# Turning keys and queries on TensorE in every batch of a top-k attention and ELU layer

## The chip, the cores and the metric

The kernel runs on one core of a Trainium2 chip. The time is device microseconds of one execution, the median over runs. The profile is of one further execution of the same program.

## The reference, cut to what matters

Attention over 8 batches, 8 heads, 576 tokens and head width 64, in which each query keeps the 32 largest of its 576 scores, and behind it a two-layer network with an ELU between (4608 tokens, widths 512, 2048, 512).

```python
scores = scale * np.matmul(q, k.transpose(0, 1, 3, 2))
kth = np.partition(scores, -top_k, axis=-1)[..., -top_k:-top_k + 1]
scores = np.where(scores >= kth, scores, -1000000000.0)
scores = scores - np.max(scores, axis=-1, keepdims=True)
attn = np.exp(scores)
attn = attn / (np.sum(attn, axis=-1, keepdims=True) + 1e-09)
attn_out = np.matmul(attn, v).astype(np.float32)
...
x = attn_out.transpose(0, 2, 1, 3).reshape(B * S, H * D)
h = x @ w_in
g = np.where(h > 0.0, h, np.exp(np.minimum(h, 0.0)) - 1.0)
return (g @ w_out).astype(np.float32)
```

## The kernel before, in words

**Steps.** Queries are taken in tiles of 128 rows, and heads in pairs. 576 rows make four tiles (`J = 4`) and a remainder of 64 rows, the "last queries", of which a step takes two head pairs at once. One step is one tile and one head pair; there are 18 steps a batch, 144 in all (`NS`). `first[b]` is the first step of batch b, here called f. `orders[b]` says in which order a batch takes its tiles; `(J,)` in it stands for the remainder.

**What a step does, by engine.** `scores` (L331) multiplies queries by keys on TensorE into two PSUM tiles `wide[0]` and `wide[1]`, and ScalarE evicts them (L348) into the tile `sc`. `select` finds the 32 largest of each row on VectorE: a MAX8 on the scores (L360), then three times MATCH_REPLACE8 (L367) and MAX8 (L374), for both heads. `mask` makes weights of them on ScalarE (L401, L402), `normalise` scales them on POOL (L412 to L417). The weights are then turned so that keys lie on partitions: in one step of three by `turn`, on TensorE (L437) with a copy by ScalarE (L438), and in the two others ("aside") by `split`, `write` and `cross`, which send 16-bit halves through a DMA transpose. `turn` puts eight of its nine chunks into the PSUM pool `ps_t` (two buffers) and the ninth into free columns of `wide[1]`. `attend` (L488) multiplies by the values and `finish` copies into `xT`.

**The network behind it** is cut into pieces (`ffn_pieces`): `hidden` (L563, evicted at L573 to L582) and `product` or `project` (L656, L591). A "gate" is the last step of the ELU, on POOL (L533) or VectorE (L535); gates are put in a list and `close_gates` issues them some pieces later. `feed`, four times a step, issues as many pieces as a budget planned from `due` allows. Strips of w_out (`tw`) are streamed from DRAM by SP (L698).

**The order of the work** is written out by hand, one program order for all engines, and each engine runs its part in order. In program step n stand: the scores of step n + 2; the selection of step n; the mask and normalise of step n - 1; the turn, or the writing of halves, of step n - 2; the cross of step n - 3. `todo` holds calls for the start of a step and `mid` for its middle.

**Keys and queries before a batch.** Scores need the head width on partitions, in a tile `kqT` (`kvpool`, five buffers). For batch 0, `load_qk` loads rows as they lie (four rows to a partition), and `transpose_qk` turns them on TensorE with nine 128x128 transposes for a head pair: the leftover rows into free columns of `wide[0]` (L299), eight chunks into `ps_t` (L310), copied by ScalarE (L302, L306, L316). For batches 1 to 7, `load_halves` (L240) loads 32-column halves, so that 32x32 blocks lie ready, and VectorE turns them with two STREAM_TRANSPOSEs (L294), each 128x576. The input tiles of these batches have one buffer each. `plan` gives, for each of the four head pairs, how many steps before f it is loaded and how many before f it is turned (`start_qk` announces it; `turn_qk` runs one part in the middle of a step and the rest at its end). `load_v` (L274, L281) loads the values.

Of the kernel before, what the change touches and what calls it, by code (L numbers as in the profile page):

```python
# [10 lines left out]
FP32 = mybir.dt.float32  # L11
# [72 lines left out]
def kernel(  # L84
# [25 lines left out]
    KEYS, QUERIES = R, R + S  # L110
    Q = 32
    NB = S // Q
    scale = 1.0 / float(D) ** 0.5
# [134 lines left out]
    def load_qk(b, hp, other=nc.sync):  # L248

        for name, src in (("k", k), ("q", q)):  # L250
            n, queue = (J + 1, nc.sync) if name == "k" else (J, other)
            t = ldpool.tile([P, n, 2, D], FP32, tag=name + "in", name=name + "in")
            if name == "k":
# [12 lines left out]
    def load_v(b, hp):  # L266

        t = kvpool.tile([P, 2 * J + 2, D], FP32, tag="vT", name="vT")
        for hh in range(2):
            h = 2 * hp + hh  # L270
            main = R * hh if b else 0
            end = JP if b == 0 else JP * (1 - hh)
            order = "(p j) d -> p j d" if b == 0 else "(j p) d -> p j d"
            nc.sync.dma_start(  # L274
                t[:, hh * J : (hh + 1) * J, :],
                v[b, h, main : main + JP, :].rearrange(order, j=J),
            )
            mine = slice(hh * R, (hh + 1) * R)
            other = slice((1 - hh) * R, (2 - hh) * R)
            nc.gpsimd.memset(t[other, 2 * J + hh, :], 0.0)  # L280
            nc.sync.dma_start(t[mine, 2 * J + hh, :], v[b, h, end : end + R, :])  # L281
        vT[b, hp] = t

    def transpose_qk(b, hp):
# [5 lines left out]
        kqT[b, hp] = d[:].rearrange("p c d -> p (c d)")  # L290
        if b > 0:
            for i, name in enumerate(("k", "q")):
# [38 lines left out]
    def scores(u):  # L331

        u.sc = scpool.tile([P, 2, S], FP32, tag="sc", name="sc")
        q0 = (QUERIES if u.t.b == 0 else S) + u.t.qt * P
        for half in range(2):
            for h, i, rows in u.heads:
                kq = kqT[u.t.b, h // 2]
                part = slice(i * D, (i + 1) * D)
                k0 = (KEYS if i == 0 and u.t.b == 0 else 0) + half * HS
                nc.tensor.matmul(  # L340
# [381 lines left out]
    for b in range(B):  # L722
# [4 lines left out]
        else:  # L727
            order = [(0,), (1, 2), (3,)]
        if b % 2 and b > 1:
            if len(order[0]) == 2:  # L730
                order = [(0,), (1,), (2, 3)]
            orders.append(order[:1] + [(J,)] + order[1:])
        else:
            orders.append([(J,)] + order if b % 2 else order + [(J,)])
        ends += [(b, qt) for qts in orders[b] for qt in qts if qt < J or b % 2]
# [7 lines left out]
    for b in range(B):  # L743
        first[b] = len(steps)
        tiles = []
        for qt in range(J + 1):
            r0 = b * S + (JP if qt == J else qt if b == 0 else qt * P)
            if qt == J:
                (blk, slot), c0, n = slots[b | 1, J], (b % 2) * R, R
                rows = slice(r0, r0 + R)  # L750
            else:
                (blk, slot), c0, n = slots[b, qt], 0, P
                rows = slice(r0, r0 + J * (P - 1) + 1, J) if b == 0 else slice(r0, r0 + P)
            c0 += slot * P
# [24 lines left out]

    todo, mid = {}, {}  # L780

# [3 lines left out]
    for b in range(1, B):  # L785
        f = first[b]
        plan = ((9, 5), (4, 3), (2, 1), (0, -1))
        if len(orders[b][0]) == 1:
            plan = ((9, 5), (4, 3), (2, 1), (0.5, 0))
        if b == 1:  # L790
            plan = ((7, 5), (4.5, 4), (3.5, 3), (2.5, 2))
        for hp, (ahead, ready) in enumerate(plan):
            if ahead % 1:
                mid.setdefault(f - int(ahead + 0.5), []).append((load_halves, (b, hp)))
            else:
                at(f - ahead, load_halves, b, hp)
            at(f - ready, start_qk, b, hp)
# [66 lines left out]
    for n in range(NS + 3):  # L864
# [39 lines left out]
        if done and done.aside:  # L904
            split(done, 0)
            write(done, 0)
        if prev:
            normalise(prev)
            if prev.aside:
                close_gates(1)  # L910
                split(prev, 1)
        if spare and n >= first[1] - 2:
            difference(*spare.pop(0))
        feed(n, 0.25)
        turn_qk(True)
        if n < 2:
            scores(ahead)
# [36 lines left out]
```

## Time and profile before

| | |
|---|---|
| median of 3 runs | 1578.12 us (1576.59 to 1578.77) |
| the profiled execution | 1579.89 us |
| its span, first to last instruction | 1577.8 us |
| granted TensorE clock, mean | 0.967 |
| busy: TensorE, VectorE, ScalarE, POOL | 1461.6, 1450.2, 1182.8, 995.4 us |
| DMA queue q1 (SP) | 447856 packets, 197.49 MB |

Times in the profile are in microseconds from the start of the span; "mean ns" is of one instruction. PE is TensorE's matmuls, PEld its weight loads, DVE VectorE, ACT ScalarE, POOL GpSimd, SP the engine that issues most DMAs. An fp32 matmul shows as two records, a transpose as one. In a group of instructions the figures are: count, busy time in all, mean of one, and the idle time of the engine just before them with what ended it. In a wait they are: time in all, number, longest. In a stretch they are the busy times of the engines with the number of instructions, the granted clock, the share of the DMA engines and GB/s.

### The profile page before, as it was taken

How to read it: one execution, taken by the hardware profiler on the slowest of the kernel's cores; microseconds unless marked ns; L12 is line 12 of the kernel's file. 1: busy time of each engine (PE TensorE's matmuls, PEld its weight loads, DVE VectorE, ACT ScalarE, POOL GpSimd, SP SyncE). 2: the span in 40 equal slices, each digit the busy share in tenths (PEclk: the TensorE clock that was granted, in tenths of full speed). 3: DMA queues.
4: the chain of work that ended last, by engine and by line, in shares of the span. 5: the costliest groups of instructions: out<-in, count | busy, mean ns of one | idle time of the engine just before them, and what ended most of it. 6: DMA issues, size and time to landing. Idle time of an engine off the chain costs nothing.

```text
span 1577.8 us, 28727 instructions
## 1 busy us (share of the span) xinstructions
PE 1461.6 (93%) x9598; PEld 1155.1 (73%) x9598; DVE 1450.2 (92%) x2976; ACT 1182.8 (75%) x2296; POOL 995.4 (63%) x1493
## 2 busy tenths in 40 slices
PE   4789989989999999998999898999999999999899
PEld 2467557657777778776777776788788778887786
DVE  6899999999999999999899989999999997999600
ACT  6897677769696868686777777687969786978542
POOL 4993466655757566757575665758666666676550
PEclk9879989999999999999999999899999999999999
DMA  8621444646757585566646475738674757563410
GB/s 236 200 82 23 92 109 132 146 113 147 210 116 204 109 191 137 155 154 146 170 137 180 109 190 128 193 81 214 132 207 98 211 115 197 116 195 95 146 55 33
DMA packets 472595, 224.98 MB, mean 143 GB/s; under 512 B 385920, under 2 KB 430976, under 8 KB 472448
## 3 DMA queue, kind: packets, MB, share of 16 engines
q1 hardware_dynamic: 447856, 197.49, 50.3%
q10 hardware_dynamic: 24592, 25.66, 4.8%
q8 instruction: 76, 1.25, 0.3%
q14 instruction: 71, 0.58, 0.1%
HBM read 108.00 MB, written 64.36 MB: 109 GB/s over the span
## 4 chain that ended last, share of the span: by engine, by line
PE 41%; ACT 25%; DVE 14%; POOL 9%; issue 6%; DMA 3%; SPq 1%; ACTq 1%; DVEq 0%; POOLq 0%
PE ops L656 18%; PE hps L563 9%; PE avps L488 6%; DVE wk L367 6%; PE scps L340 5%; DVE m L374 5%; ACT sc L402 4%; ACT sc L401 4%; ACT n L573 3%; ACT n L578 3%; ACT sc L348 3%; ACT gT L576 2%; ACT n L582 2%; POOL sc L417 2%; ACT planes L454 2%
## 5 line engine op out<-in xcount | busy, mean ns | idle before, releaser
L374 DVE MAX8 m<-wk 128x8 f32<-128x576 f32 x864 | 607.8, 743 | 0.0
L563 PE MATMUL hps<-xT,w_in 128*128 128x256 f32 (+1 forms) x2688 | 541.0, 357 | 0.9 <-ACT xT L515 0.7
L563 PEld LDWEIGHTS hps<-xT,w_in 128*128 128x128 f32 x2688 | 452.8, 194 | 69.3 <-issue 19.8
L367 DVE MATCH_REPLACE8 wk<-m,wk 128x576 f32<-128x576 f32 x576 | 422.3, 739 | 0.0
L402 ACT ACTIVATE sc<-sc,den 128x576 f32<-128x576 f32 x288 | 223.4, 776 | 91.4 <-POOL den L381 78.1
L417 POOL TENSOR_SCALAR sc<-sc,den 128x576 f32<-128x576 f32 x288 | 236.2, 827 | 15.0
L401 ACT ACTIVATE sc<-sc,m 128x576 f32<-128x576 f32 x288 | 223.1, 775 | 26.8 <-DVE m L374 26.8
L412 POOL TENSOR_SCALAR den<-den 128x2 f32<-128x2 f32 x144 | 32.6, 226 | 331.8 <-ACT sc L402 329.2
L656 PE MATMUL ops<-tw,gT 128*128 128x256 f32 x960 | 224.9, 387 | 17.5 <-POOL gT L533 10.3
L340 PE MATMUL scps<-kqT 64*128 64x288 f32 (+1 forms) x1280 | 203.7, 449 | 39.3 <-ACT et L438 19.7
L656 PEld LDWEIGHTS ops<-tw,gT 128*128 128x128 f32 x960 | 179.5, 191 | 52.4 <-POOL gT L533 12.6
L360 DVE MAX8 m<-sc 128x8 f32<-128x576 f32 x288 | 201.6, 740 | 12.4 <-ACT sc L348 11.8
L367 DVE MATCH_REPLACE8 wk<-m,sc 128x576 f32<-128x576 f32 x288 | 211.0, 739 | 0.0
L348 ACT ACTIVATE sc<-scps 128x576 f32<-128x576 f32 x288 | 171.1, 647 | 51.0 <-PE scps L340 26.5
L533 POOL TENSOR_TENSOR gT<-n,gT 128x512 f32<-128x512 f32 x136 | 173.3, 1276 | 54.7 <-ACT n L582 53.7
L488 PEld LDWEIGHTS avps<-et,vT 128*64 128x64 f32 x3200 | 167.5, 142 | 44.6 <-issue 31.8
L488 PE MATMUL avps<-et,vT 128*64 128x128 f32 (+1 forms) x3200 | 190.7, 274 | 5.5 <-ACT et L438 5.4
L340 PEld LDWEIGHTS scps<-kqT 64*128 64x128 f32 (+1 forms) x1280 | 109.1, 184 | 108.6 <-issue 30.4
L656 PE MATMUL ops<-w_out,gT 128*128 128x256 f32 x720 | 175.1, 399 | 0.0
L656 PEld LDWEIGHTS ops<-w_out,gT 128*128 128x128 f32 x720 | 143.1, 202 | 24.7 <-issue 3.1
L609 POOL TENSOR_TENSOR gT<-gT 128x1024 f32<-128x1024 f32 x60 | 141.9, 2366 | 21.8 <-PE ops L656 20.5
L573 ACT ACTIVATE n<-hps 128x512 f32<-128x512 f32 x144 | 85.0, 591 | 55.7 <-PE hps L563 37.0
(57 smaller groups left out, 1486.3 us busy)
## 6 DMA issues: line engine op xcount, KB each, us to landing
tw<-kept SPq DMA_DIRECT2D x240, 256.0 KB, 3.5
halves<-planes ACTq DMA_DIRECT2D x86, 288.0 KB, 2.9
halves<-planes SPq DMA_DIRECT2D x86, 288.0 KB, 2.9
raw<-in_moe_w_in_dram SPq DMA_DIRECT2D x16, 512.0 KB, 5.4
vT<-in_v_dram SPq DMA_DIRECT2D x64, 128.0 KB, 2.9
raw<-in_moe_w_out_dram SPq DMA_DIRECT2D x16, 512.0 KB, 4.1
out_dram<-osb SPq DMA_DIRECT2D x32, 256.0 KB, 3.1
kin<-in_k_dram SPq DMA_DIRECT2D x112, 72.0 KB, 2.8
```

The source lines that it names most:

```text
L340: nc.tensor.matmul(wide[i][rows, half, 0:HS], kq[part, q0 : q0 + u.t.ql], kq[part, k0 : k0 + HS], start=True, stop=True,)
L348: nc.scalar.activation(u.sc[:, i, :].rearrange("p (a s) -> p a s", a=2), wide[i][:, :, 0:HS], AF.Copy, scale=scale,)
L360: nc.vector.max(found[i], cur[i])
L367: nc.vector.match_replace(wk[i], found[i], cur[i], TAKEN)
L374: nc.vector.max(found[i], cur[i])
L401: nc.scalar.activation(sc, sc, AF.Prelu, scale=-1.0, bias=low, alpha=1.0 / STEEP)
L402: nc.scalar.activation(sc, sc, AF.Exp, scale=-STEEP, bias=gap, accum_out=u.den[:, i : i + 1])
L417: nc.gpsimd.tensor_scalar(u.sc[:, i, :], u.sc[:, i, :], rec[:, i : i + 1], den[:, i : i + 1], ALU.mult, ALU.mult,)
L488: nc.tensor.matmul(ps[i * D : (i + 1) * D, cols], vt[:, 2 * J + i if c == J else i * J + c, :], w, start=(c == 0), stop=(c == J),)
L533: nc.gpsimd.tensor_tensor(dst, n, dst, ALU.add)
L563: nc.tensor.matmul(blk.h[:, f % bank, :], w_in[:, i, f * P : (f + 1) * P], blk.xT[:, i, 0:n_tok], start=(i == 0), stop=(i == NC - 1),)
L656: nc.tensor.matmul(sums, x[:, f, :], w, start=opens and f == 0, stop=f == NG - 1, skip_group_check=not opens,)
```

## The change

Keys and queries of all batches are loaded by `load_qk` as rows and turned by `transpose_qk` on TensorE; VectorE turns none. A set `by_pe` holds the batches that are treated so, here all. The tile of the loads comes from the pool that the late batches use, with one buffer for each of the two tensors. With it go:

- Keys now stand in another order (four neighbouring rows to a partition), so values are loaded in that order too, and a tile's output rows have a stride of four.
- The plan of loads and turns becomes (8, 6), (6, 4), (4, 2), (2, 0) steps before f for the four head pairs, and loads are issued at the end of their step, by a new table `behind`, after the turns of that step. In batch 1 the first load stands in the middle of a step.
- In batch 1 the remainder comes second, as it does in the other odd batches.
- In all steady steps `close_gates(1)` is called ahead of `normalise`; before it was called behind it, and only in steps that go aside.

```diff
+    by_pe = set(range(B))
...
     def load_qk(b, hp, other=nc.sync):
 
+        keep = late["in"] if b else ldpool
         for name, src in (("k", k), ("q", q)):
             n, queue = (J + 1, nc.sync) if name == "k" else (J, other)
-            t = ldpool.tile([P, n, 2, D], FP32, tag=name + "in", name=name + "in")
+            t = keep.tile([P, n, 2, D], FP32, tag=name, name=name + "in")
...
-            main = R * hh if b else 0
-            end = JP if b == 0 else JP * (1 - hh)
-            order = "(p j) d -> p j d" if b == 0 else "(j p) d -> p j d"
+            main = 0 if b in by_pe else R * hh
+            end = JP if b in by_pe else JP * (1 - hh)
+            order = "(p j) d -> p j d" if b in by_pe else "(j p) d -> p j d"
...
-        if b > 0:
+        if b not in by_pe:
             for i, name in enumerate(("k", "q")):
                 src = loaded.pop((b, hp, name))[:].rearrange("p n d -> p (n d)")
                 nc.vector.transpose(kqT[b, hp][:, i * S : (i + 1) * S], src)
...
-        if b % 2 and b > 1:
+        if b % 2:
             if len(order[0]) == 2:
                 order = [(0,), (1,), (2, 3)]
             orders.append(order[:1] + [(J,)] + order[1:])
         else:
-            orders.append([(J,)] + order if b % 2 else order + [(J,)])
+            orders.append(order + [(J,)])
...
-                rows = slice(r0, r0 + J * (P - 1) + 1, J) if b == 0 else slice(r0, r0 + P)
+                rows = slice(r0, r0 + P)
+                if b in by_pe:
+                    rows = slice(r0, r0 + J * (P - 1) + 1, J)
...
-        plan = ((9, 5), (4, 3), (2, 1), (0, -1))
-        if len(orders[b][0]) == 1:
-            plan = ((9, 5), (4, 3), (2, 1), (0.5, 0))
+        plan = ((8, 6), (6, 4), (4, 2), (2, 0))
         if b == 1:
-            plan = ((7, 5), (4.5, 4), (3.5, 3), (2.5, 2))
+            plan = ((7.5, 6), (6, 4), (4, 2), (2, 0))
         for hp, (ahead, ready) in enumerate(plan):
+            load = load_qk if b in by_pe else load_halves
             if ahead % 1:
-                mid.setdefault(f - int(ahead + 0.5), []).append((load_halves, (b, hp)))
+                mid.setdefault(f - int(ahead + 0.5) + 1, []).append((load, (b, hp)))
             else:
-                at(f - ahead, load_halves, b, hp)
+                behind.setdefault(f - ahead, []).append((load, (b, hp)))
...
         if prev:
+            if steady:
+                close_gates(1)
             normalise(prev)
             if prev.aside:
-                close_gates(1)
                 split(prev, 1)
...
         turn_qk(True)
+        for fn, args in behind.pop(n, []):
+            fn(*args)
```

More of the change, by code (lines that the diff above doesn't have):

```diff
@@ L333, in scores @@
         u.sc = scpool.tile([P, 2, S], FP32, tag="sc", name="sc")
-        q0 = (QUERIES if u.t.b == 0 else S) + u.t.qt * P
+        q0 = (QUERIES if u.t.b in by_pe else S) + u.t.qt * P
         for half in range(2):
@@ L338, in scores @@
                 part = slice(i * D, (i + 1) * D)
-                k0 = (KEYS if i == 0 and u.t.b == 0 else 0) + half * HS
+                k0 = (KEYS if i == 0 and u.t.b in by_pe else 0) + half * HS
                 nc.tensor.matmul(
@@ L746 @@
         for qt in range(J + 1):
-            r0 = b * S + (JP if qt == J else qt if b == 0 else qt * P)
+            r0 = b * S + (JP if qt == J else qt if b in by_pe else qt * P)
             if qt == J:
@@ L778 @@
             u.group.due = n + 4 + u.aside
-    todo, mid = {}, {}
+    todo, mid, behind = {}, {}, {}
     def at(step, fn, *args):
```

## The prediction

> **What bounds the kernel now.** I read the page first: busy shares, then the chain that ended last.
>
> ```profile
> span 1577.8 us, 28727 instructions
> PE 1461.6 (93%) x9598; PEld 1155.1 (73%) x9598; DVE 1450.2 (92%) x2976; ACT 1182.8 (75%) x2296; POOL 995.4 (63%) x1493
> PE 41%; ACT 25%; DVE 14%; POOL 9%; issue 6%; DMA 3%; SPq 1%; ACTq 1%; DVEq 0%; POOLq 0%
> ```
>
> TensorE and VectorE are equally full over the span, so the shares do not say which one sets the pace. Busy time by stage does; I cut the stages at the first MAX8 of a step (L360).
>
> ```profile
> 1322.89:1477.13 154.24, 150.09 (x1067) 123.53 (x1066) 154.24 (x322) 123.53 (x246) 104.85 (x158) 1.00 0.55 150
> 713.35:722.99 9.64, 9.64 (x90) 8.09 (x88) 9.64 (x21) 7.35 (x15) 6.80 (x11) 1.00 0.16 44
> 702.39:713.35 10.96, 7.90 (x47) 5.67 (x47) 10.96 (x23) 10.09 (x20) 5.52 (x9) 1.00 0.61 125
> 1304.34:1322.89 18.55, 18.55 (x123) 15.23 (x122) 11.20 (x23) 11.92 (x24) 15.17 (x20) 1.00 0.91 229
> ```
>
> The columns are PE, PEld, DVE, ACT, POOL, clock, DMA share, GB/s. The first row is sixteen steps without a transpose (20 VectorE instructions in each): VectorE is busy for all 154.24 us, 9.64 a step, as in the single step of the second row. The third row is a step with one pair of STREAM_TRANSPOSEs: 10.96, so a pair costs 1.32. In the fourth a pair also waits for its load: 18.55 us, of which VectorE works 11.20. The groups by line and shape give the totals:
>
> ```profile
> L294 DVE STREAM_TRANSPOSE kqT<-kin 128x576 f32<-128x576 f32 x28 | 21.2, 757 | 12.3 <-DMA kin<-in_k_dram 12.3
> L294 DVE STREAM_TRANSPOSE kqT<-qin 128x576 f32<-128x576 f32 x28 | 20.7, 740 | 9.9 <-DMA qin<-in_q_dram 9.8
> ```
>
> So VectorE sets the pace, but how far behind it is TensorE? I measured the lead: from the end of a step's score eviction (L348, two instructions in one row) to that step's first MAX8. These rows of the timeline are of steps 91 and 119:
>
> ```profile
> 927.98 1.19 ACT L348 ACTIVATE sc<-scps 128x576 f32<-128x576 f32 x2 [0.58 <-PE scps L340]
> 956.79 1.40 DVE L360 MAX8 m<-sc 128x8 f32<-128x576 f32 x2
> 1219.12 1.17 ACT L348 ACTIVATE sc<-scps 128x576 f32<-128x576 f32 x2
> 1232.14 1.40 DVE L360 MAX8 m<-sc 128x8 f32<-128x576 f32 x2
> ```
>
> Step 91 has its scores 956.79 - 929.17 = 27.6 us early, step 119 only 1232.14 - 1220.29 = 11.9. In those 28 steps VectorE took 9.83 us a step (275.4/28) and the producers of scores 10.40 (291.1/28). VectorE lives there on a stock of finished scores; its wait in the 18.55 us step fills the stock again. A kernel that takes these waits away therefore meets TensorE next. Its own demand:
>
> ```profile
> 131.81 1.24 PE L340 MATMUL scps<-kqT 64*128 64x288 f32 x8
> 1457.42 1.24 PE L340 MATMUL scps<-kqT 64*128 64x288 f32 x8
> 131.80:1457.40 1325.60, 1257.63 (x8443) 997.35 (x8442) 1302.78 (x2680) 1024.54 (x1972) 856.37 (x1307) 0.97 0.59 147
> 1034.04:1283.50 249.46, 245.59 (x1635) 201.15 (x1634) 249.44 (x513) 202.40 (x390) 170.03 (x252) 0.99 0.61 153
> 1486.86:1577.80 90.94, 87.18 (x482) 71.75 (x479) 2.77 (x4) 33.71 (x68) 26.57 (x25) 0.99 0.12 38
> ```
>
> Between the scores of step 12 (131.81) and of step 143 (1457.42) lie 131 steps, with 9.60 us of busy TensorE each (1257.63/131). The next row is 25 steps, from the scores of step 101, in which the lead was short: TensorE 98.4% busy, clock 0.99 against 0.97 over the long stretch. In the last, after VectorE's end, TensorE drains what is left.
>
> **What goes from VectorE.** 28 pairs by 1.32 = 37.0 us, and the waits for loads, 12.3 + 9.8 = 22.1. Together 59.1: by VectorE alone the span would be 1577.8 - 59.1 = 1518.7.
>
> **What comes to TensorE and ScalarE.** Each of the 28 head pairs of batches 1 to 7 now needs nine 128x128 transposes and four copies.
>
> ```profile
> L437 PE MATMUL eps<-ident,sc 128*128 128x128 f32 x464 | 75.2, 288 | 13.9 <-POOL sc L417 13.2 <-ACT xT L515 0.7
> L437 PEld LDWEIGHTS eps<-ident,sc 128*128 128x128 f32 x464 | 58.3, 148 | 31.6 <-POOL sc L417 21.0 <-issue 2.2 <-ACT xT L515 1.7
> L310 PE MATMUL qkps<-ident,kin 128*128 128x128 f32 x16 | 4.2, 421 | 0.0
> L316 ACT COPY kqT<-qkps 128x512 f32<-128x512 f32 x8 | 4.5, 599 | 1.5 <-PE qkps L310 1.5
> L302 ACT COPY kqT<-scps 128x128 f32<-128x128 f32 x4 | 1.0, 259 | 2.4 <-PE scps L299 2.3
> L306 ACT COPY kqT<-scps 128x64 f32<-128x64 f32 x4 | 0.9, 220 | 0.0
> ```
>
> TensorE: 252 transposes. The same operation in the steady part (L437) adds 75.2/464 = 0.162 us each, so 40.8 us. Bounds: 58.3/464 = 0.126 by its weight loads (31.7), 4.2/16 = 0.26 as batch 0 runs it at the cold start (66). I take 0.162, the row of the steady part. ScalarE: 28 x (2 x 0.599 + 0.259 + 0.220) = 47.0 us. In the long stretch it was busy 1024.5 of 1325.6 us (77%); with 47 more in a shorter stretch some 83%. It has the room, but it works in order, and these copies queue behind the mask of the step before, which waits for VectorE.
>
> **New waits on TensorE.** The four transposes of keys and of queries use the two ps_t buffers that attend and turn use; the ninth (the leftover rows) goes into bank wide[0], which the scores of the same step fill and ScalarE must empty first. Behind that transpose stand the step's other PE work and the next scores. The nearest rows are the single-chunk turn into wide[1] and what the score matmuls wait for:
>
> ```profile
> PE scps L437 <- ACT sc L348: 23.1, 18, 1.9
> L437 PE MATMUL scps<-ident,sc 128*128 128x128 f32 x58 | 18.3, 316 | 24.2 <-ACT sc L348 23.1 <-POOL sc L417 0.8
>   ACT et L438: 44.9, 22
>   DVE kqT L294: 10.7, 3
> ```
>
> The first two say that 18 of the 58 single-chunk turns waited, 23.1 us in all, 0.40 a turn: 28 x 0.40 = 11.2 us. From the other side, the last line is what scores waited for VectorE's transposes, 10.7, and that goes. The two about cancel: +0.5. Ends: -10.7 if no turn waits; if each waits as the 18 did, 1.28, it is 28 x 1.28 - 10.7 = +25.
>
> **Loads.** Per head pair, eight transfers become six, issued at the end of a step (behind what that step queued on SP) two steps ahead of their turn, where the last pair had half a step.
>
> ```profile
> kin<-in_k_dram SPq DMA_DIRECT2D x112, 72.0 KB, 2.8
> kin<-in_k_dram SPq DMA_DIRECT2D x8, 128.0 KB, 4.8
> L256 SPq DMA_DIRECT2D kin<-in_k_dram x8: 549/629/851, 0.7 to 18.6; - x8
> SPq L240 <- DVE kqT L294: 27.2, 3, 16.0
> ```
>
> Issue takes 6 x 0.63 = 3.8 us on SP, landing 4.8 by the row loads of batch 0: 8.6, against one and a half steps (14.5). So I cost the loads at nothing; what hides them is the step between. With one input buffer each, SP can be held at a load until the last pair is turned, as it was 27.2 us in three places; the w_out strips and score halves are queued behind. If the cover is gone, the 22.1 us of waits fall on TensorE instead.
>
> **The smaller edits.** The gates now close ahead of the normalise in every steady step. POOL has time there, and a gate's input (L582) stands ahead of the mask on ScalarE:
>
> ```profile
> POOL den L412 <- ACT sc L402: 329.2, 116, 6.7
> L533 POOL TENSOR_TENSOR gT<-n,gT 128x512 f32<-128x512 f32 x136 | 173.3, 1276 | 54.7 <-ACT n L582 53.7
> ```
>
> POOL waits 329.2 us for the mask before its normalise; the gate falls into that wait. Taken at 0; at worst a normalise is 1.28 us later, which the lead covers, and at best the halves leave 1.28 earlier. In batch 1 the two leftover steps move behind four others: the same instructions, and pair 3 is turned two steps before its use; 0. Values load in key order and rows store with a stride, the same number of transfers; 0.
>
> **Sum.** TensorE: 1257.6 + 40.8 = 1298.4 of busy time between the two score groups. VectorE needs 131 x 9.64 = 1262.8 for those steps, less, so TensorE is the later one now. It should then run as in the 25 short-lead steps: 1298.4 x 0.97/0.99 = 1272.2 at their clock, over 0.984 (245.59/249.46) = 1292.9. Before it lie 131.8 us, behind it 1577.8 - 1457.4 = 120.4, unchanged since TensorE has the same work there and was busy for 87.18 of the last 90.94. 131.8 + 1292.9 + 120.4 + 0.5 = 1545.6 of span. The profiled execution took 1579.89, 2.1 over its span, and the median of the runs is 1578.12, so 0.3 over the span: 1546. By this sum 59 us are released on VectorE and some 32 arrive.
>
> **The rivals.**
> First, TensorE has the room and VectorE stays the bound. TensorE's busy time holds modelled ends of matmuls that nothing needs, and steps in which it waited for VectorE anyway; weight loads were busy only 1155.1 of 1577.8 us. Then all 59.1 arrive: 1518.7 + 0.3 = 1519. Against it: 10.40 against 9.83 in steps 91 to 119. The Trainium skill (Perfetto Trace Analysis, Identifying the Most-Contended Engine) says that matmul busy time is no good measure and that weight-load busy time is one: by that rule TensorE at 73% has headroom, and the time would be this rival's. The trace agrees in part: weight loads are 81% (201.15/249.46) even where the lead shrinks, so that TensorE is short of time before this measure is full.
> Second, slower: the turn holds TensorE at wide[0]. The ninth transpose waits for an eviction that stands behind ScalarE's other work, and the next scores wait until ScalarE has copied it out. Price per turn: 1.28 for the first and, in half of them, 44.9/22 = 2.04 for the second, together 2.30. The sum then has 28 x 2.30 = 64.4 in place of 0.5: 1610. It decides from (1577.8 - 1545.1)/28 = 1.17 us a turn. For it: ScalarE at 83%, in order. Against it: 40 of 58 single-chunk turns did not wait.
> Third, the change does not do what it says because the loads are late for TensorE as they were for VectorE: +22.1, 1568. SP's 27.2 speaks for it, the 14.5 us against it.
> Fourth, the clock falls in the transposes. At batch 0's 421 ns against 288 the 252 cost 40.8 x 421/288 = 59.6, so 1565. Against it are the 464 transposes at 288 between matmuls. The Trainium skill (TensorE: Matmul & The Clock Gate, Part 4: PE-mode transpose) holds that transposes do not count as activity for the clock gate, which speaks against the change; the 464 show no such loss.
>
> **How the numbers follow.** Forecast 0.52, room on TensorE 0.22, late loads 0.07, clock 0.03, slower at wide[0] 0.16. What a measurement of this kernel can tell is about 0.2%, 3.2 us. Of the rival at wide[0] I give 0.13 to slower and 0.03 to no change (about 1.17 us a turn); of the forecast's own spread 0.02 goes to no change. Faster 0.50 + 0.22 + 0.07 + 0.03 = 0.82, same 0.05, slower 0.13. The range goes from 1519 (the room on TensorE, which has too much chance to be left out) up past late loads and the forecast with every turn waiting (1546 + 25 = 1571, or 1546 + 66 - 40.8 = 1571 with the dear transposes) to no gain: 1519 to 1580.
>
> **What would show it.** Right: no STREAM_TRANSPOSE on VectorE and no waits for kin; steps of 9.64 without the 10.96 and 18.55 in the first half; a lead that shrinks to a few us, and MAX8 (L360) waiting for L348 in the last third; 252 more transposes at about 0.16; PE busy between 1476 (1461.6 + 40.8, at the better clock) and 1502, over 95% of the span; ScalarE busy near 1230. A lead that stays over 10 us to the end shows the first rival. Wrong: VectorE idle from batch 2 on behind scores, with TensorE waiting for L348 or for the copies of kqT by over 1.2 us a turn, or waits of TensorE for kin and qin; or PE busy over 1530.

## The result, and the profile after

The changed kernel takes 1583.36 us (median, 1580.81 to 1588.44) against 1574.46 us (1571.95 to 1578.77) for the kernel before in the runs beside it: ratio 1.0066, 95% interval 1.0053 to 1.0078. It is slower by some 10 us by the ratio; the forecast was 1546, faster by 2% than the 1578.12 us that it started from. The profiled execution took 1583.26 us, its span is 1581.4. From here on lines are those of the changed kernel; most stand two below those of before (scores L342, eviction L350, first MAX8 L362, mask L403 and L404, turn L439; the new turn is L301 and L312, with its copies at L304, L308 and L318).

The page after, first the busy shares, then the chain that ended last:

```profile
span 1581.4 us, 29155 instructions
PE 1473.1 (93%) x9850; PEld 1175.5 (74%) x9850; DVE 1415.2 (89%) x2920; ACT 1216.7 (77%) x2412; POOL 997.6 (63%) x1493
PE 47%; ACT 30%; POOL 10%; issue 6%; DVE 3%; DMA 2%; SPq 1%; ACTq 1%; POOLq 0%
```

VectorE has lost 35 us of work and has gone from the chain (14% before, 3% now). But its place was not taken by TensorE alone: ScalarE stands in the chain with 30% where it had 25%, though it is busy for only 77% of the span.

Stretches of the span (same columns as in the prediction). The first row is the stretch from the scores of step 12 to those of step 143, as it was quoted of before; the next two are VectorE's steps 11 to 73 and 74 to 143, cut where it first has to wait, the last is what lies behind VectorE's end:

```profile
131.80:1459.40 1327.60, 1267.30 (x8695) 1016.46 (x8694) 1283.71 (x2656) 1058.36 (x2088) 858.54 (x1307) 0.99 0.55 147
143.73:751.22 607.49, 578.13 (x4105) 455.75 (x4105) 607.46 (x1261) 487.92 (x962) 392.01 (x608) 0.99 0.55 146
751.22:1473.46 722.24, 688.78 (x4609) 563.49 (x4608) 678.37 (x1401) 571.57 (x1128) 474.70 (x707) 0.98 0.57 151
1473.46:1581.40 107.94, 101.73 (x590) 84.38 (x588) 2.77 (x4) 43.75 (x91) 33.83 (x41) 0.97 0.20 62
```

In the second row VectorE is busy for 607.46 of 607.49 us: 63 steps of 9.64, as forecast. In the third row it idles for 722.24 - 678.37 = 43.9 us, and 70 steps take 10.32 each. VectorE ends 13.4 us earlier than before (1473.46 against 1486.86), but what lies behind its end is 17.0 us longer (107.94 against 90.94). That is not new work: from the last scores to the end of the span it takes 122.0 us where it took 120.4. VectorE now ends 14.1 us after the last scores begin where it ended 29.4 us after them, since its stock is gone, and the last scores themselves come no earlier (1459.4 against 1457.4).

How the stock of finished scores is used up can be seen in the timeline, by a step's eviction (two instructions in one row) and the MAX8 that reads it, here for steps 20 and 75:

```profile
208.57 1.19 ACT L350 ACTIVATE sc<-scps 128x576 f32<-128x576 f32 x2 [0.62 <-PE avps L490]
230.49 1.41 DVE L362 MAX8 m<-sc 128x8 f32<-128x576 f32 x2
...
762.69 1.19 ACT L350 ACTIVATE sc<-scps 128x576 f32<-128x576 f32 x2 [2.37 <-PE scps L342]
763.38 1.42 DVE L362 MAX8 m<-sc 128x8 f32<-128x576 f32 x2 [2.44 <-ACT sc L350]
```

Step 20 has its scores 230.49 - 209.76 = 20.7 us early; in step 75 VectorE starts as soon as the first of the two evictions has ended, having waited 2.44 us. That the lead would go was expected. The surprise is in what TensorE itself then waits for (waits: total, number, longest):

```profile
PE scps L342 <- ACT kqT L318: 30.3, 9, 8.4
PE scps L342 <- ACT et L440: 15.2, 9, 2.4
PE scps L301 <- ACT sc L350: 15.0, 10, 3.7
PE scps L439 <- ACT sc L350: 14.8, 13, 2.3
DVE m L362 <- ACT sc L350: 43.2, 20, 11.9
POOL gT L535 <- ACT n L584: 173.2, 71, 8.7
```

The four largest waits of TensorE are all for ScalarE. The two largest of the kernel before were so too (23.1 us at the single-chunk turn, 19.7 for the copy `et`); the first and the third row, all but 1.5 us of the latter, are what has come. In the first row, four waits with 12.3 us lie in the start-up; 18.0 us in five waits are new: the scores wait for the copy that hands over their own keys. Here is one of the five, in the timeline:

```profile
218.28 0.60 ACT L575 ACTIVATE n<-hps 128x512 f32<-128x512 f32 x1 [0.62 <-ACT planes L456]
218.78 0.59 ACT L578 ACTIVATE gT<-hps 128x512 f32<-128x512 f32 x1
219.25 0.63 ACT L580 ACTIVATE n<-n 128x512 f32<-128x512 f32 x1
219.92 0.63 ACT L584 ACTIVATE n<-n 128x512 f32<-128x512 f32 x1
220.45 0.57 ACT L318 COPY kqT<-qkps 128x512 f32<-128x512 f32 x1
221.07 2.29 PE L342 MATMUL scps<-kqT 64*128 64x288 f32 x8 [6.21 <-ACT kqT L318]
```

The copy takes 0.57 us, but it stands behind four instructions of the network's ELU, and these behind a half of the weights (L456); TensorE is idle for 6.21 us. ScalarE is not full; it has a line, and TensorE waits for something at the line's end.

### The profile page after: what moved, and what is told of

It is laid out like the page before. It is cut to its first block, busy times and chain, and to the rows that moved or that the text cites. A ratio compares the mean times of both kernels' runs of the same rounds, so it can differ in the third digit from the quotient of the medians.

```text
span 1581.4 us, 29155 instructions
## 1 busy us (share of the span) xinstructions
PE 1473.1 (93%) x9850; PEld 1175.5 (74%) x9850; DVE 1415.2 (89%) x2920; ACT 1216.7 (77%) x2412; POOL 997.6 (63%) x1493
## 3 DMA queue, kind: packets, MB, share of 16 engines
q1 hardware_dynamic: 360944, 197.48, 47.3%
## 4 chain that ended last, share of the span: by engine, by line
PE 47%; ACT 30%; POOL 10%; issue 6%; DVE 3%; DMA 2%; SPq 1%; ACTq 1%; POOLq 0%
PE ops L658 18%; PE hps L565 13%; PE avps L490 6%; PE scps L342 6%; ACT sc L404 5%; ACT sc L403 5%; ACT n L575 3%; ACT n L580 3%; ACT sc L350 3%; ACT gT L578 3%; ACT n L584 3%; POOL sc L419 2%; PE ops L593 2%; ACT planes L456 2%; POOL den L415 2%
## 5 line engine op out<-in xcount | busy, mean ns | idle before, releaser
L565 PE MATMUL hps<-xT,w_in 128*128 128x256 f32 (+1 forms) x2688 | 546.7, 359 | 0.6 <-ACT xT L517 0.6
L404 ACT ACTIVATE sc<-sc,den 128x576 f32<-128x576 f32 x288 | 223.4, 776 | 85.4 <-POOL den L383 71.7
L362 DVE MAX8 m<-sc 128x8 f32<-128x576 f32 x288 | 202.9, 747 | 49.9 <-ACT sc L350 43.2
L342 PE MATMUL scps<-kqT 64*128 64x288 f32 (+1 forms) x1280 | 203.1, 450 | 46.2 <-ACT kqT L318 30.3
L403 ACT ACTIVATE sc<-sc,m 128x576 f32<-128x576 f32 x288 | 224.0, 778 | 2.1 <-DVE m L376 2.1
L658 PE MATMUL ops<-tw,gT 128*128 128x256 f32 x960 | 221.1, 384 | 3.9 <-DMA tw<-kept 3.2
L350 ACT ACTIVATE sc<-scps 128x576 f32<-128x576 f32 x288 | 171.4, 649 | 52.0 <-PE scps L342 33.1
L342 PEld LDWEIGHTS scps<-kqT 64*128 64x128 f32 (+1 forms) x1280 | 109.9, 185 | 110.1 <-ACT kqT L318 33.1
L658 PE MATMUL ops<-w_out,gT 128*128 128x256 f32 x720 | 165.2, 383 | 0.0
L658 PEld LDWEIGHTS ops<-w_out,gT 128*128 128x128 f32 x720 | 135.5, 191 | 21.6 <-issue 4.0
L575 ACT ACTIVATE n<-hps 128x512 f32<-128x512 f32 x144 | 85.4, 593 | 63.2 <-PE hps L565 43.1
```

What stands on the lines that cost most here:

```text
L342: nc.tensor.matmul(wide[i][rows, half, 0:HS], kq[part, q0 : q0 + u.t.ql], kq[part, k0 : k0 + HS], start=True, stop=True,)
L350: nc.scalar.activation(u.sc[:, i, :].rearrange("p (a s) -> p a s", a=2), wide[i][:, :, 0:HS], AF.Copy, scale=scale,)
L362: nc.vector.max(found[i], cur[i])
L403: nc.scalar.activation(sc, sc, AF.Prelu, scale=-1.0, bias=low, alpha=1.0 / STEEP)
L404: nc.scalar.activation(sc, sc, AF.Exp, scale=-STEEP, bias=gap, accum_out=u.den[:, i : i + 1])
L565: nc.tensor.matmul(blk.h[:, f % bank, :], w_in[:, i, f * P : (f + 1) * P], blk.xT[:, i, 0:n_tok], start=(i == 0), stop=(i == NC - 1),)
```

## The experiments

The first four runs were to decide between three theories. **The bank:** the ninth transpose, into `wide[0]`, holds TensorE (the prediction's second rival). **Plain work:** only the 41 us of transposes count. **The gates:** closing them ahead of the normalise is the loss. When none of them fitted all four, two more came in. **ScalarE's line:** the 47 us of copies lengthen ScalarE's in-order line; what stands behind them comes late, evictions above all, and TensorE, which no longer has VectorE's slack in front of it, waits. **The handing over:** the scores wait for the copy of their own keys. All ratios are to the kernel before, with 95% intervals; 0.1% is about 1.6 us. The kernel before was timed anew beside each group of runs (its medians lie between 1574.46 and 1580.7 us), so kernels are compared by their ratios.

**1. The turn taken out** (`no_turn`). The loads, the gates and the new order stay.

```diff
+        if b > 0:
+            kqT[b, hp] = kqT[0, hp]
+            yield
+            return
         d = kvpool.tile([P, 4 * J + 3, D], FP32, tag="kqT", name="kqT")
```

> The changed kernel without the turn in batches 1 to 7: their scores use batch 0's turned keys and queries, loads stay. Bank theory (each turn holds TensorE some 1.6 us at wide[0], beside 41 us of transposes): both go, 1583 - 41 - 45 is under VectorE's own bound, so VectorE sets the time, 1519 to 1530. Plain work theory (only the 41 us of transposes count): about 1542. Gate theory (closing gates ahead of the normalise ties POOL to TensorE and is the loss): no better than 1555, since the gates stay.

Measured: 1538.63 us, ratio 0.9756 (0.9726 to 0.9786). Against the changed kernel's 1.0066 the turn costs 3.1%, some 49 us: more than the 40.8 us of TensorE's transposes if every one of them stood on the path. Of the three expectations the 1542 of plain work is nearest; the bank theory's 1519 to 1530 is not reached.

**2. The ninth transpose taken out** (`no_ninth`). In batches 1 to 7 the two small copies read the first chunk's PSUM tile; `wide[0]` is not used by the turn.

```diff
-        ps = wide[0][:, 1, HS : HS + P]
-        nc.tensor.transpose(
-            ps, srcs[0][:, J, :, :].rearrange("p h d -> p (h d)"), ident[:]
-        )
+        if b == 0:
...
+            if b > 0 and i == 0:
+                rest(ps[:, 0:P])
```

> The changed kernel without the ninth transpose in batches 1 to 7: the two small copies read the first chunk's PSUM tile instead of wide[0], so 64 leftover rows hold other rows' values. Bank theory: TensorE no longer waits for the eviction of wide[0], 28 x 1.2 to 1.6 us go, 1540 to 1552. Plain work theory: 28 x 0.16 = 4.5 us go, 1578. Gate theory: the same 1578.

Measured: 1587.95 us, ratio 1.0067 (1.0041 to 1.0094), the same as with the ninth. TensorE's waits in this kernel (its lines are six below those of the changed kernel):

```profile
PE scps L348 <- ACT kqT L324: 30.6, 9, 9.0
PE scps L445 <- ACT sc L356: 21.1, 17, 2.4
PE eps L445 <- ACT kqT L324: 6.3, 5, 2.3
PE scps L309 <- ACT sc L356: 1.5, 2, 0.7
```

The wait at the ninth transpose is gone (15.0 us in 10 in the changed kernel, 1.5 in 2 of the start-up now), and others for ScalarE have grown by nearly as much: the single-chunk turn from 14.8 to 21.1, a wait of the turn for the copy of the keys from 0.6 to 6.3. Part of the latter may come from the edit itself, since the two small copies now read a buffer of `ps_t`. The bank theory falls, and experiment 5 speaks against it too: there the wait at `wide[0]` stays (13.4 us in 10) and the kernel is faster than the one before. By these rows the wait is a place at which TensorE notices that ScalarE is late; without it TensorE notices later.

**3. The gates put back** (`gates_back`), where the kernel before had them.

```diff
-            if steady:
-                close_gates(1)
             normalise(prev)
             if prev.aside:
+                close_gates(1)
                 split(prev, 1)
```

> The changed kernel with close_gates(1) where it was: behind the normalise and only in steps that go aside. Gate theory: 1583 falls by 10 us or more. Bank theory and plain work theory: within 4 us of 1583.

Measured: 1600.47 us, ratio 1.0158 (1.0123 to 1.0193). The gate theory, by which this gains 10 us or more, falls: the edit that the prediction took at 0 is worth 0.9%, about 14 us, in the changed kernel.

**4. VectorE turns** (`dve_turn`), with the new gates, loads as early and the new order.

```diff
-    by_pe = set(range(B))
+    by_pe = {0}
```

> The changed kernel with by_pe = {0}: VectorE turns batches 1 to 7 again, with the changed plan of loads and turns, the gates and the order of batch 1 as changed. Bank and plain work theories: VectorE pays 28 x 1.32 = 37 us but no longer the 22 us of waits for loads, TensorE pays nothing: 1574.5 - 22 = 1552, at best. Gate theory: the gates hold it back, 1570 or more.

Measured: 1568.57 us, ratio 0.9937 (0.991 to 0.9963). All of the change but the turn, and the loads and the key order that belong to it, makes the kernel faster by 0.6%. That is between the two expectations, 1552 at best and 1570 or more.

**5, 6 and 9. The turn's parts alone.** `pe_only` keeps the 252 transposes and leaves the copies out; `act_only` keeps the copies, out of the loaded rows in SBUF, and leaves the transposes out; `act_aside` is `act_only` with the copies going to a spare tile that nobody reads, while the scores use batch 0's keys.

```diff
+        if b > 0:
+            flat = [x[:].rearrange("p n h d -> p (n h d)") for x in srcs]
+            nc.scalar.copy(d[:, 2 * J + 1 : 4 * J + 3 : 2 * J + 1, :], ...flat[0]...)
+            nc.scalar.copy(d[:, 0, :], flat[0][:, 0:R])
+            for i in range(2):
+                c0 = KEYS + i * (2 * J + 1) * D
+                nc.scalar.copy(kqT[b, hp][:, c0 : c0 + JP], flat[i][:, 0:JP])
+                yield
+            return
```

> The changed kernel with the 252 transposes of batches 1 to 7 but without the four copies a pair: scores use batch 0's turned keys and queries. Between no turn at all (1538.6) and the changed kernel (1583). TensorE-work theory: the transposes are the price, 41 us at most: 1570 to 1583. ScalarE theory (the price is 47 us of copies in ScalarE's queue, which delays the evictions that TensorE waits for): 1540 to 1555. Handing-over theory (the price is that scores wait for the last copy of a pair, 18 us of waits for kqT): about 1565.

> The changed kernel with the four copies a pair but without the transposes in batches 1 to 7: ScalarE copies the loaded rows as they lie, from SBUF, so keys and queries are not turned. TensorE-work theory: 1538 to 1545. ScalarE theory: 1570 or more. Handing-over theory: some 1555, since scores still wait for the last copy.

> The kernel act_only again, but its four copies a pair go to a spare tile that nobody reads; scores use batch 0's turned keys and queries, there are no transposes in batches 1 to 7. The same ScalarE time as act_only, and no score waits for a copy. ScalarE theory (47 us of copies delay everything behind them in ScalarE's queue): near act_only, 1575 to 1589. Handing-over theory (the loss is that scores wait for the copy of their own keys): near no turn at all, 1539 to 1548.

| kernel | in it, of the turn | us | ratio | over `no_turn` |
|---|---|---|---|---|
| `no_turn` | nothing | 1538.63 | 0.9756 (0.9726 to 0.9786) | |
| `pe_only` | transposes | 1556.87 | 0.9842 (0.9813 to 0.987) | 0.9%, 14 us |
| `act_aside` | copies that nobody waits for | 1566.92 | 0.9919 (0.9893 to 0.9944) | 1.6%, 26 us |
| `act_only` | copies that the scores wait for | 1589.16 | 1.0053 (1.0018 to 1.0089) | 3.0%, 47 us |
| changed | all | 1583.36 | 1.0066 (1.0053 to 1.0078) | 3.1%, 49 us |

The copies alone cost nearly what the whole turn costs; the transposes alone cost less than a third of it. The copies cost in two ways: 26 us when nobody waits for them, and 21 more as soon as somebody does. The 26 lie between what the two theories expected (36 to 50 us over `no_turn`, and at most 9), so each is right in part. The waits of TensorE in `act_only` show the second part; `act_aside` has no such row:

```profile
PE scps L354 <- ACT kqT L309: 28.8, 5, 8.3
PE scps L451 <- ACT sc L362: 24.5, 17, 2.4
PE scps L354 <- ACT et L452: 20.7, 13, 3.5
```

L309 is the copy of the keys: five waits, 28.8 us. The intervals of such differences are some 0.4% wide either way, so the third and the fourth row differ surely, but the parts add up only roughly (0.9% and 3.0% make more than 3.1%).

Waiting is not all that the copies cost. In the stretch from the scores of step 12 to those of step 143 (us, from the profiles):

| kernel | stretch | TensorE busy | idle | clock |
|---|---|---|---|---|
| `no_turn` | 1284.3 | 1239.3 | 45.0 | 0.99 |
| `pe_only` | 1301.5 | 1258.2 | 43.3 | 0.99 |
| `act_aside` | 1313.0 | 1249.6 | 63.4 | 0.98 |
| `act_only` | 1333.1 | 1253.9 | 79.2 | 0.97 |
| changed | 1327.6 | 1267.3 | 60.3 | 0.99 |

`act_only` has 34.2 us more of idle time than `no_turn`, and 14.6 us more of busy time for the same matmuls, at a lower granted clock; for `act_aside` it is 18.4 and 10.3. The mean clock was lower in each of their runs (0.960 to 0.972) than in any of `no_turn` and `pe_only` (0.977 to 0.981). Whether the waits bring the clock down was not tested. The changed kernel's clock did not fall, so the two costs are not to be carried over to it one by one.

**7. Copies earlier** (`whole_mid`): both parts of a turn in the middle of its step, where one stood in the middle and one at the end.

```diff
-            turn_qk()
+            turn_qk(True)
```

> The changed kernel with both halves of a pair's turn in the middle of the step (turn_qk(True) there), so that the copy of the queries stands ahead of the second mask on ScalarE. Handing-over theory: most of the 18 us of waits for kqT go, 1565 to 1572. TensorE-work theory: 1583 within 4. ScalarE theory: 1583 within 4, or slower, as more copies stand ahead of the mask.

Measured: 1583.74 us, ratio 1.0028 (1.0005 to 1.0051). By the ratio that is some 6 us better than the changed kernel, but the times (1583.74 and 1583.36) and the stretches between the two score groups (1328.4 and 1327.6) are the same, so that a gain is not shown; 1565 to 1572 was expected for the handing over. The wait of the scores for the keys goes from 30.3 us in 9 to 13.1 in 5, little more than the start-up's; but the turn of the weights now waits for the copy:

```profile
PE scps L342 <- ACT kqT L318: 13.1, 5, 8.7
PE eps L439 <- ACT kqT L318: 12.4, 6, 4.0
```

Two thirds of what went from the first came back in the second, because both use the two buffers of `ps_t`. A better place for the copies is not enough.

**8. A POOL step moved** (`spread_dve`): the difference at L383, on which the mask waits 71.7 us, computed by VectorE.

```diff
-        nc.gpsimd.tensor_tensor(
+        nc.vector.tensor_tensor(
             u.den[:, 2:4], u.last[:, :, 7], u.first[:, :, 0], ALU.subtract
```

> The changed kernel with the small subtraction `spread` (128x2) on VectorE instead of POOL, so that ScalarE's second mask no longer waits behind POOL's gates (71.7 us of waits in 45 places). If ScalarE's lag is what holds TensorE: 1555 to 1570. TensorE-work theory: 1583 within 4, plus up to 144 x 0.07 = 10 us where VectorE is the bound.

Measured: 1595.56 us, ratio 1.0085 (1.0056 to 1.0115). This says nothing on ScalarE's line, since VectorE paid for it: 136 instructions of two columns raised its busy time from 1415.2 to 1464.9 us, where some 10 us had been expected (the last section shows why).

**10. ScalarE relieved** (`pool_split`): both halves of every `split` on POOL, which had one of them. It takes 86 copies of 1138 ns, 97.9 us, from ScalarE and gives them to POOL.

```diff
-        copy = nc.gpsimd.tensor_copy if i else nc.scalar.copy
+        copy = nc.gpsimd.tensor_copy
```

> The changed kernel with both halves of `split` on POOL: 97.9 us less on ScalarE, 98 more on POOL (63% busy before). ScalarE theory: the time falls to where TensorE's work or VectorE set it, 1545 to 1565. TensorE-work and handing-over theories: no gain, 1580 to 1595, since POOL only gets later.

Measured: 1550.51 us, ratio 0.9822 (0.9797 to 0.9848): 2.4% under the changed kernel, 1.8% under the one before. Nothing of the turn is altered. The page, the stretch between the same two score groups, and TensorE's waits:

```profile
PE 1461.5 (94%) x9850; PEld 1167.2 (75%) x9850; DVE 1414.1 (91%) x2920; ACT 1127.2 (73%) x2326; POOL 1092.1 (71%) x1579
PE 55%; POOL 14%; ACT 12%; DVE 12%; issue 4%; DMA 1%; SPq 1%; ACTq 1%; POOLq 0%; DVEq 0%
131.10:1425.70 1294.60, 1256.89 (x8695) 1009.10 (x8694) 1283.40 (x2661) 971.09 (x2004) 951.28 (x1393) 0.99 0.57 151
PE scps L301 <- ACT sc L350: 5.9, 4, 2.6
PE scps L439 <- ACT sc L350: 1.4, 3, 0.6
DVE m L362 <- ACT sc L350: 16.7, 6, 11.7
PE scps L342 <- ACT kqT L318: 23.7, 9, 9.3
```

ScalarE's part of the chain falls from 30% to 12%, TensorE's waits for evictions from 29.8 us (15.0 + 14.8) to 7.3, and VectorE's for scores from 43.2 to 16.7, with one wait of the start in both (11.9 and 11.7). The wait of the scores for their keys shrinks less, from 30.3 to 23.7, of which 12.4 are the start-up's: 11.3 us of the 18.0 are still there. The stretch takes 1294.60 us, 33.0 less than in the changed kernel; 22.6 of them are idle time, the rest is shorter busy time for the same matmuls.

**11. Fewer turns on TensorE** (`mix2`): batches 0 to 2 on TensorE, 3 to 7 on VectorE; keys and queries share one input tile, so that both layouts fit.

```diff
-    by_pe = set(range(B))
+    by_pe = {0, 1, 2}
...
+            both = late["in"].tile([P, 2 * S], FP32, tag="kq", name="kqin")
```

> The changed kernel with batches 1 and 2 turned on TensorE and 3 to 7 on VectorE. By the runs so far VectorE's turn costs at least 5.3 us a batch on its own bound of 1519 (1545 with five batches) and the turn by TensorE and ScalarE 6.3 to 7 a batch on 1539 (1553 with two): 1553 to 1562, faster than all batches on VectorE (1568.6) if the two bounds add up from separate engines; 1570 or more if both are one chain.

Measured: 1556.9 us, ratio 0.9854 (0.9829 to 0.9878), 2.1% under the changed kernel: with fewer turns on TensorE the loss goes as well.

**12. The gates alone in the kernel before** (`before_gates`): the reverse of the diff of experiment 3, and nothing else of the change.

```diff
+            if steady:
+                close_gates(1)
             normalise(prev)
             if prev.aside:
-                close_gates(1)
                 split(prev, 1)
```

> The kernel before with nothing changed but close_gates(1) ahead of the normalise in all steady steps. In the changed kernel this edit is worth 17 us (1600.5 against 1583). If it shortens a chain that VectorE's pace hides in the kernel before: within 5 us of 1576. If it is worth the same everywhere: 1558.

Measured: 1567.33 us, ratio 0.9925 (0.9897 to 0.9954). One of the change's smallest edits gains 0.75%, about 12 us, by itself, between the two expectations; `dve_turn`, with the new plan of loads and the new order of batch 1 as well, is no better. In the waits POOL's gate has gone into the time that POOL spent on the mask:

```profile
POOL den L412 <- ACT sc L402: 213.5, 114, 6.8
POOL gT L533 <- ACT n L582: 135.1, 62, 5.4
```

These were 329.2 and 53.7 before.

**13 to 16. Was ScalarE's line there before?** It was open whether the 2.4% of `pool_split` belong to the turn or would have come in any kernel. `before_pool` is `before_gates` with the edit of `pool_split`, `dve_pool` is `dve_turn` with it, `mix2_pool` is `mix2` with it, `pool_mid` is `whole_mid` with it. In all four:

```diff
-        copy = nc.gpsimd.tensor_copy if i else nc.scalar.copy
+        copy = nc.gpsimd.tensor_copy
```

> The kernel before with the early gates and with both halves of every split on POOL, so 98 us of work fewer on ScalarE; VectorE turns the keys as before. My theory: ScalarE's order costs time only where TensorE sets the pace; here VectorE sets it in most steps, so the move is worth at most a third of the 24 permille that it was worth in the changed kernel: ratio to before 0.985 to 0.9925 (gates alone 0.9925). Rival: ScalarE was at fault whoever turns the keys; then the same 24 permille come off: 0.968 to 0.972, and the changed turn stays a loss also when ScalarE is relieved.

> The changed kernel with VectorE turning the keys of batches 1 to 7 (new loads, gates and order kept) and both halves of every split on POOL. My theory: as the run before it, 0.985 to 0.9937, so slower than the 0.9822 of the same relief with TensorE's turn. Rival: 0.968 to 0.972.

> TensorE turns the keys of batches 0 to 2, VectorE those of 3 to 7, and both halves of every split are on POOL. My theory: the two remedies overlap, since both take work off ScalarE or TensorE where it sets the pace, and VectorE comes in as the bound in the last five batches (20 pairs of 1.32 are 26 us): 0.976 to 0.982. Rival (ScalarE at fault throughout): the two add up, 0.9822 x 0.9854 / 1.0066 = 0.9615, less what VectorE then holds back.

> The changed kernel with both halves of every split on POOL and both parts of each turn in the middle of its step. Alone the second edit was worth 3.8 permille. My theory: the handing over of the keys still waits in ScalarE's line, less than before, so half of that remains: 0.979 to 0.982. Rival: once ScalarE has room the place of the copies does not matter: 0.982 to 0.984.

| who turns batches 1 to 7 | split as it was | split on POOL | worth |
|---|---|---|---|
| VectorE, kernel before with the gates | 0.9925 (0.9897 to 0.9954) | 0.9873 (0.9844 to 0.9902) | 0.5% |
| VectorE, changed kernel | 0.9937 (0.991 to 0.9963) | 0.9899 (0.9871 to 0.9927) | 0.4% |
| TensorE 1 and 2, VectorE 3 to 7 | 0.9854 (0.9829 to 0.9878) | 0.9811 (0.9779 to 0.9843) | 0.4% |
| TensorE | 1.0066 (1.0053 to 1.0078) | 0.9822 (0.9797 to 0.9848) | 2.4% |
| TensorE, copies in the middle | 1.0028 (1.0005 to 1.0051) | 0.9893 (0.986 to 0.9927) | 1.4% |

The same 98 us off ScalarE are worth 0.4 to 0.5% as long as VectorE turns most of the keys, about as little as these intervals can tell from nothing, and 2.4% when TensorE does. The chain of `before_pool` says who sets the pace there:

```profile
DVE 49%; PE 29%; POOL 7%; ACT 6%; issue 5%; DMA 3%; SPq 1%; ACTq 0%; DVEq 0%; POOLq 0%
```

So ScalarE's line was there before and VectorE covered it. The change took the cover away and made the line longer by the copies; which of the two weighs more is not shown, since `no_turn` was not run with the split on POOL. `pool_mid` missed: 1564.51 us, slower than `pool_split`, where 0.979 to 0.982 were expected. Its turn of the weights waits for the copies of the keys (14.8 us in 6, against 1.1 in 3 in `pool_split`), as in `whole_mid`. But TensorE's idle time between the two score groups is the same as in `pool_split` (39.6 us against 37.7), and of the 15.2 us by which that stretch is longer 13.3 are busy time for the same matmuls, at a granted clock of 0.98 against 0.99. So in these profiles the miss comes with the clock and not with idle time, and what the place of the copies is worth is not shown. The two fastest versions that turn all their keys, `pool_split` (1550.51 us) and `mix2_pool` (1550.92 us), cannot be told apart, and both beat the kernels before and after. `pool_split` differs from the changed kernel by one expression.

## Why the prediction was wrong, step by step

- **VectorE bounds the kernel before, at 9.64 us a step without a transpose:** right. 63 steps in a row took 9.64 after the change (607.46 of 607.49 us busy), and 35 us left VectorE.
- **The stock of scores runs out and TensorE comes next:** the order was right. The lead was gone at 751 us, half way, where the prediction looked for it in the last third. Two of its signs came out against it: VectorE idles behind the scores, from step 74 on, and TensorE is busy for 1473.1 us, 93% of the span, where 1476 to 1502 and over 95% stood for right.
- **252 transposes at 0.162 us:** right by the rows: the 256 chunk transposes at L312 took 43.1 us, 0.168 each. What they add to TensorE's busy time is less: in `pe_only` the stretch has 18.9 us more of it than in `no_turn`, at the same clock of 0.99, where the sum had 40.8; why was not found out. The rows are from the groups by shape:

```profile
L312 PE MATMUL qkps<-ident,kin 128*128 128x128 f32 x128 | 21.9, 299 | 0.7 <-ACT xT L517 0.7
L312 PE MATMUL qkps<-ident,qin 128*128 128x128 f32 x128 | 21.2, 293 | 0.3 <-ACT et L440 0.2
L318 ACT COPY kqT<-qkps 128x512 f32<-128x512 f32 x64 | 37.5, 591 | 8.4 <-ACT planes L456 4.4 <-PE qkps L312 1.5 <-PE eps L439 1.2
```

- **TensorE's busy time of 1272.2 us between the two score groups, at a clock of 0.99:** right as a number, 1267.30 at 0.99. In part that is luck: without the turn it was 1239.3 (`no_turn`), where the sum implies 1257.6 x 0.97/0.99 = 1232.2, and the whole turn added 28.0, where it had 40.
- **It then runs with 1.6% idle, 1292.9 us for the stretch:** this is the step that failed. The stretch took 1327.60 us, of which 60.3 are idle, 4.5%, where the sum had 20.7. The miss is these 39.6 us, less the 4.9 that TensorE was busy for less: 34.7. Behind the stretch lie 122.0 us for a forecast of 120.4, and the 0.5 us of new waits is part of the idle time now: 34.7 + 1.6 - 0.5 = 35.8, which is 1581.4 - 1545.6. The share of 1.6% came from 25 steps of a kernel in which VectorE still had scores in stock and ScalarE none of the copies; it was carried to a kernel in which both were otherwise. Over the whole long stretch the kernel before had 1325.60 - 1257.63 = 68.0 us of idle time; the sum took 47.3 of them away, the change took 7.7.
- **"It has the room", ScalarE's 47.0 us of copies at 0:** the main reason for that failure. Its size was forecast well enough (busy 1216.7 us for some 1230; instructions that follow closely overlap in these records, so that 34 of the 47 show) and its effect was not: the copies alone cost 47 us (`act_only`, some 15 of it as slower matmuls). The prediction wrote that ScalarE works in order and that the copies queue behind the mask, and gave it no price in the sum. With the copies left out, the stretch takes 1301.5 us (`pe_only`), with ScalarE relieved 1294.60 (`pool_split`), against the 1292.9 that the sum had for it: of the 34.7 us of the miss 26.1 go with the copies. That both totals come so near is luck in part: 43.3 and 37.7 us of them are idle, not 20.7, at 14 and 15 us less of busy time. An idle share of 1.6% came in none of these runs, not even with no turn at all (45.0 us, 3.5%, in `no_turn`, where VectorE is busy for all but 3.2 us of the stretch and may itself have held TensorE). So the share was too small also without the copies, and what fills that part stays open.
- **New waits at `wide[0]`, +0.5 (-10.7 to +25):** the wait appeared, 15.0 us in 10 (1.5 of them in the start-up), while the waits for VectorE's transposes went, so the net is within the bounds. The prediction's 10.7 adds the waits of matmuls, 6.9, and of weight loads, 3.8; TensorE's matmuls were spared only 6.9. Removing the cause of the new wait gained nothing (`no_ninth`). The dear wait, of the scores for the copy of their keys, was priced nowhere: the prediction counted only that "pair 3 is turned two steps before its use". In the step quoted above TensorE waits 6.21 us for such a copy.
- **Loads at nothing:** right in so far as no wait for a load larger than the start-up's appears on TensorE. With VectorE turning, the early loads did not gain beyond the gates (0.9937 against 0.9925).
- **Gates at 0:** wrong, and in the kernel's favour: 0.75% alone, 0.9% in the changed kernel. Without it the change would have been slower by 1.6%. The prediction had found the wait of POOL into which the gate falls and gave no price to its end.
- **The rivals.** The slower one had the sign and the engine pair, the wrong place, and a price that was too high: 64.4 us of waits on top of 40.8 of transposes, 1610, where the whole turn cost 49. Room on TensorE (1519) did not come. The Trainium skill (Perfetto Trace Analysis, Identifying the Most-Contended Engine) has TensorE's headroom judged by the share of weight loads among others, which spoke for this rival. That share is 77% in the stretch after (1016.46/1327.60) and 78% in `pool_split` (1009.10/1294.60), whose time is still 30 us above the rival's, so these runs do not bear it out as the room that is left. Late loads did not show. Nor did a clock that falls in the transposes: the mean was 0.976 after and 0.967 before, and with the transposes alone 0.980 (`pe_only`) where it was 0.978 without them (`no_turn`).

## What to carry to other kernels

When the engine that sets the pace is relieved, look not only at how full the next one is but at what that one waits for: each in-order engine that feeds it may have been covered by the old bound, and a stretch in which the old bound still stood ahead cannot show what it will cost. ScalarE at 77% had no room for work that another engine waits for, because that work stood at the end of its line; price the copy by the line ahead of it, not by its own 0.6 us. And take a change apart into its edits: here a small reordering gained 12 to 14 us, while the turn cost 49 us on TensorE and ScalarE (1.0066 - 0.9756) where it had cost 28 on VectorE (0.9937 - 0.9756).

## What was not expected of the hardware

A short instruction on VectorE can last as long as an instruction of POOL. By the mean, the 128x2 subtraction at L383 seems dear on VectorE, 375 ns against 200 on POOL (136 of them in each profile):

```profile
L383 POOL TENSOR_TENSOR den<-m,m 128x2 f32<-128x2 f32 x136 | 27.2, 200 | 5.5 <-DVE m L376 5.5
L383 DVE TENSOR_TENSOR den<-m,m 128x2 f32<-128x2 f32 x136 | 51.0, 375 | 14.8 <-POOL den L416 0.5 <-DVE m L376 0.5
568.07 2.35 POOL L611 TENSOR_TENSOR gT<-gT 128x1024 f32<-128x1024 f32 x1
568.35 2.08 DVE L383 TENSOR_TENSOR den<-m,m 128x2 f32<-128x2 f32 x1
```

The first row is of the changed kernel, the others of `spread_dve`. But the median on VectorE is 163 ns, and 84 of the 136 took 0.16 us. In the last two rows the subtraction begins while POOL's instruction runs and ends with it (570.43 and 570.42 us). 32 of the 136 took over 0.5 us, and 29 of these ended within 0.03 us of the end of a POOL instruction that was under way when they began. That reads as VectorE waiting for POOL inside its own instruction, where the list of waits does not show it.

The copy of a half of the weights took the same time on POOL as on ScalarE, 1143 and 1138 ns, so POOL got no more work than ScalarE was spared.
